# Projection stage of a transformer block on one core: PSUM pool layout, timing of the token statistics, spacing of staged loads, and staging tiles in two chunks

## The chip, the cores and the metric

The kernel runs as one program on one core of a Trainium2 chip. The metric is the device time of an execution in microseconds (us); three runs of the kernel before took 2074.11 to 2076.02 us, median 2075.82. The profile is one further execution, recorded by the hardware profiler. The engines are named as in the profile: PE (TensorE, matmul), PEld (its weight loads), DVE (VectorE), ACT (ScalarE), POOL (GpSimd), and SP, whose queue issues most of the DMA transfers. A "q" behind an engine's name (SPq, POOLq) is its instruction queue.

## The reference

A pre-norm transformer block on 2048 tokens of 640 features, 32 heads of 20, with a SwiGLU feed-forward part of 1728, all in float32:

```python
x = A_x
h = x + _A_ref(_layernorm(x, axis=-1), A_wqkv, A_wo)
h2 = h + _B_ref(_layernorm(h, axis=-1), B_w_gate, B_w_up, B_w_down)
```

`_A_ref` projects to q, k and v, takes softmax(q k^T / sqrt(20)) v for each head and multiplies by `wo`; `_B_ref` is (silu(z w_gate) * (z w_up)) w_down.

## The kernel before

**Stages.** The program has three stages in a row: the projections to q, k and v (up to 357 us), attention, and the feed-forward part with the output. The change edits the first one only. Tokens are worked off in four chunks of 512 (c = 0 to 3; the title's "chunks 2 and 3" are c = 1 and 2 here). To keep float32 accuracy, each operand is split into a high and a low part (`split`: ACT copies the high part, DVE or POOL subtracts), and each product is the sum of three products of such parts.

**Slots.** In each chunk the loop over `work` runs 18 slots (j = 0 to 17; slot number 18c + j): ten blocks of 128 columns of q or k (`query_key`), and eight half tiles of v (`value`). In chunk 0 the first two blocks are made together (`first_blocks`), and slot 1, `("none",)`, closes the first PSUM pools and opens others. A block is 15 matmuls, each cut into two halves of 64 rows of the array (`rounds`). The second half of a matmul is issued LAG = 19 matmuls behind its first half, so that first and second halves of different matmuls lie side by side on the array. At the start only first halves are there, at the end only second ones ("lone halves" in the text).

**From PSUM to DRAM.** A finished block is taken out of its PSUM bank by `keep`: before slot 10 ACT and DVE split it directly, later ACT copies it (line 605) into a staging tile e, POOL forms a difference of columns for keys (607), ACT makes the high part (85), POOL the low part (86), and a DMA stores it (500), issued by SP or, from slot 10 on, by POOL. `next_e` hands out the staging tiles in turn: two own ones and one in the space of `v_stk[0]`; in chunk 0, up to slot 10, also the two tiles that chunk 1's z will take. Values go through `keep_value` (649).

**Tokens of the next chunk.** `load_x(c)` issues four loads of 128 x 640 on SP (line 316). `norm(c)` returns 15 steps on DVE: four statistics (121, 122), seven pairs of small operations for the reciprocal root (95), four applications (460). The list `lns` is worked off one step at a time, at the ends of slots and in `visit`, which is called after each matmul of a block. From slot 11 or 12 on `flip` transposes the normalised tokens on PE and splits them into z.

**Maxima.** Softmax needs the largest score of each row ahead of attention. A part of these maxima is computed between the projections' matmuls: `max_four` (PE line 208, ReLU on ACT 220, maxima on DVE 230) from staged pieces of q and k, `max_pair` (188, 194) from the resident ones. The pieces come back from DRAM with `load_items` (DMA at line 148) into six tiles. PSUM holds 8 banks: before slot 1 two for the first blocks (`ps_one`) and three pairs for transposes (`ps_wide`); after it five for maxima and transposes (`ps_max`) and three for blocks (`ps_one`).

**What sets the order.** Each engine works off its instructions in the order in which they are written. A planner in the kernel chooses that order: `clock` holds an estimated time for each engine in ns, `takes` advances it, and `visit` writes the next step of maxima, of a split or of `lns` when these clocks allow. A staged load counts as landed LANDING = 8000 ns (12000 in early slots) after its issue on this clock. The clock is the planner's own guess and no measurement.

Of the kernel before, what the change touches and what calls it, by code (L numbers as in the profile page):

```python
# [9 lines left out]
F32 = mybir.dt.float32  # L10
# [7 lines left out]
P = 128  # L18
# [7 lines left out]
CH = 512  # L26
NC = S // CH
# [17 lines left out]
def tile_block(ctx: ExitStack, tc: tile.TileContext, x, wqkv, wo, wg, wu, wd, out):  # L45
# [22 lines left out]

    const = ctx.enter_context(tc.tile_pool(name="const", bufs=1))
    ps_ctx = ExitStack()  # L70
    psum = ps_ctx.enter_context(tc.tile_pool(name="psum", bufs=1, space=bass.MemoryType.PSUM))

    def ps_wide():
        return psum.tile([P, 2, CH], F32, name="ps_wide", tag="ps_wide", bufs=3)

    def ps_one():
        return psum.tile([P, CH], F32, name="ps_one", tag="ps_one", bufs=2)

    ident = const.tile([P, P], F32, name="ident")
    make_identity(nc, ident)  # L80
# [226 lines left out]
    with tc.tile_pool(name="pa", bufs=2) as pa:  # L307
# [18 lines left out]
        slot = [0]  # L326
# [14 lines left out]
        def load_items():  # L341
            for n, (which, g, c, loaded, _) in enumerate(items):
                if loaded is not None:
                    continue
                if slot[0] < stored_at(which, g, c) or (n >= 6 and users[n - 6]):
                    return
                if n % 6 >= 4:
                    t = more[n % 6 - 4]
                else:
                    t = raw_tile().rearrange("p a b -> p (a b)")[:, : 2 * CH].rearrange(  # L350
                        "p (h n) -> p h n", h=2
                    )
                stack(t, which, g, c, slice(CH // 2, EW) if which else slice(0, CH))
                items[n][3:] = t, clock["PE"] + (LANDING if slot[0] > 23 else LANDING_FIRST)
# [50 lines left out]
        early += staged(0, (2, 1), (2, 0))  # L405

        seconds, steps_due = [], [0]
        LANDING, LANDING_FIRST, SLACK, GATE = 8000, 12000, 0, 500

        def visit():  # L410

            load_items()
            pe = clock["PE"]
            if seconds and seconds[0][0] <= pe + SLACK:
                seconds.pop(0)[1]()
                return
            if splits and splits[0][0] <= pe and clock["ACT"] <= pe + 200:
                splits.pop(0)[1]()
            if steps_due[0] and lns and clock["DVE"] <= pe + 100:
                steps_due[0] -= 1  # L420
                lns.pop(0)()
            if held[1][0] > pe + SLACK or clock["ACT"] > pe + GATE:
                return
            for queue in (early, urgent) if slot[0] < 57 else (urgent, early):
                if queue and queue[0][0]():
                    last = queue.pop(0)[1]()
                    if last:
                        seconds.append(last)
                    return
# [245 lines left out]
        for m, raw in enumerate(first_raw):  # L675
# [1 line left out]
            nc.vector.tensor_tensor(  # L677
                out=w_lo[:, :, cs], in0=raw, in1=w_hi[:, :, cs].bitcast(F32), op=ALU.subtract
            )
        load_x(1)  # L680
        load_w(4)
        loaded = 5
        split_at = (0, 4, 6, 7, 8, 9, 10, 11, 12, 13)
# [6 lines left out]
        for c in range(NC):  # L690
            lns = []
            work = (some_keys + some_queries if c else first) + parts
            if c == NC - 1:
                work = some_keys + parts + some_queries

                es[:] = [e for e in es if e is not third]
                es.insert(1, z_tiles(NC)[0][:, :2])
            for j, (kind, *which) in enumerate(work):
                slot[0] = 18 * c + j
                if c == 0 and j < 9:  # L700
                    for i in range(split_at[j], split_at[j + 1]):
                        split_w(i + 2)
                        if i % 2 == 1 and loaded < 8:
                            load_w(loaded)
                            loaded += 1
                if (c, j) == (0, 0):
                    es[:0] = [
                        t.rearrange("p k n -> p (k n)")[:, : 2 * EW].rearrange(
                            "p (i n) -> p i n", i=2
                        )  # L710
                        for t in z_tiles(1)
                    ]
                if (c, j) == (0, 10):
                    es[:] = [e for e in es if any(e is own for own in own_es)]
                if j == 0 and c + 1 < NC:
                    if c > 0:
                        load_x(c + 1)
                    lns = norm(c + 1)
                if which:
                    if (c, j) == (0, 0):  # L720
                        first_blocks((0, 1), (1, 0), (1, 1), (0, 2), (1, 2))
                        for m, ps in enumerate(firsts):
                            keep(0, m, ps)
                    else:
                        (query_key if kind == "block" else value)(c, *which)
                else:
                    ps_ctx.close()
                    ps_ctx = ExitStack()
                    psum, psum_jobs = (
                        ps_ctx.enter_context(  # L730
                            tc.tile_pool(name=name, bufs=n, space=bass.MemoryType.PSUM)
                        )
                        for name, n in (("psum_p", 5), ("psum_j", 3))
                    )

                    def ps_one():
                        return psum_jobs.tile([P, CH], F32, name="ps_one", tag="ps_one")

                    def ps_max():
                        return psum.tile([P, CH], F32, name="ps_max", tag="ps_max")  # L740

                if c == 0 and j == 6:
                    for ev in evs:
                        nc.gpsimd.memset(ev, 1.0)
                if j == (5 if c == 0 else 4):
                    load_keys(0, slice(c * CH, (c + 1) * CH))
                if j == (5 if c == 0 else 9) and c < 3:
                    load_queries(c)
                if 0 in ends:
                    finish_at = min(finish_at, slot[0] + 2)  # L750
                    if slot[0] == finish_at:
                        max_finish(0)
                if j == 15 and c == 3:
                    load_values(0)
                if slot[0] < 9:
                    for _ in range(2 if j >= 5 else 1):
                        if j >= 1 and lns:
                            lns.pop(0)()
                else:
                    while steps_due[0] and lns:  # L760
                        steps_due[0] -= 1
# [1073 lines left out]
```

## Time and profile before

| what | us |
|---|---|
| median of three runs | 2075.82 |
| the profiled execution | 2072.07 |
| its span in the trace | 2070.1 |
| PE busy | 2031.9 (98%) |
| DVE busy | 1637.2 (79%) |
| ACT busy | 1437.0 (69%) |
| POOL busy | 745.3 (36%) |
| first / last projection matmul (line 527) starts | 26.0 / 356.2 |
| first matmul of attention (line 1127) starts | 357.3 |

How to read it: the trace lists instructions by engine with start, duration, source line, the tile written and the tiles read, the shape, and, where the engine idled before, for how long and which instruction released it. Buffer numbers are left out of names, so `e` is any of the staging tiles `e0`, `e1`. "Granted clock" is the share of full speed that PE was given; where it is 0.5, matmuls take twice as long and PE still counts as busy. Windows give busy time of each engine by stretch. Line numbers are those of the kernel before; behind the first edits the changed kernel's are higher by 4 to 13.

### The profile page before, as it was taken

Reading aid. Unit: us, or ns where it says so; the run is one execution under the profiler, and the core shown is the slowest. Engines: PE = TensorE matmul, PEld = TensorE weight load, DVE = VectorE, ACT = ScalarE, POOL = GpSimd, SP = SyncE. Lnnn points to the kernel's source line nnn. Section 1 sums busy time; section 2 is a strip of 40 time slices with the busy share of each in tenths; the row PEclk is TensorE's granted clock in tenths of the full one; section 3 lists DMA queues with packets and bytes.
Section 4 is the critical chain, followed back from the end, with each engine's and each line's share of the span. In section 5 each row is a group of like instructions: output and inputs, shape, how many; then the busy total and the mean of one; then the engine's idle time right before and its main releaser. Section 6 shows DMA issues by size and latency. Waiting matters only on the chain.

```text
span 2070.1 us, 39666 instructions
## 1 busy us (share of the span) xinstructions
PE 2031.9 (98%) x14198; PEld 1257.6 (61%) x14198; DVE 1637.2 (79%) x2895; ACT 1437.0 (69%) x2835; POOL 745.3 (36%) x1042
## 2 busy tenths in 40 slices
PE   7989999999999999999999999999999999999999
PEld 6878998333333333333333333345588888888888
DVE  6767777888888888888888888886368666676677
ACT  3647866999999999999999999996733222212221
POOL 2353533234344253344310010001145444754555
PEclk9999999999999999999999999999999999999999
DMA  6756744153443443534522113132138765884542
GB/s 208 245 186 204 217 149 134 44 177 107 144 131 121 154 132 104 186 118 164 159 86 75 36 47 95 30 109 63 32 132 304 238 193 166 320 290 160 198 150 96
DMA packets 192172, 305.53 MB, mean 148 GB/s; under 512 B 47440, under 2 KB 82256, under 8 KB 190952
## 3 DMA queue, kind: packets, MB, share of 16 engines
q1 hardware_dynamic: 185272, 278.34, 42.2%
q0 software_dynamic: 6608, 24.65, 3.8%
q8 instruction: 113, 1.85, 0.4%
q14 instruction: 83, 0.68, 0.1%
q10 hardware_dynamic: 96, 0.00, 0.0%
HBM read 203.82 MB, written 98.30 MB: 146 GB/s over the span
## 4 chain that ended last, share of the span: by engine, by line
PE 89%; DMA 4%; DVE 3%; POOL 1%; ACT 1%; issue 1%; SPq 1%; ACTq 0%; DVEq 0%; POOLq 0%
PE acc L1137 25%; PE ps_one L1127 16%; PE ps_a L1298 15%; PE ps_max L241 12%; PE ps_b L1392 8%; PE ps_one L527 7%; PE ps_max L208 2%; PE ps_max L858 2%; PE ps_b L858 1%; DMA halves<-j_d 1%; DVE mx L194 1%; DMA q_d<-e 1%; DMA xt<-in_A_x 1%; DMA units<-w_d 0%; DMA k_d<-v_stk 0%
## 5 line engine op out<-in xcount | busy, mean ns | idle before, releaser
L1133 ACT ACTIVATE probs<-ps_one 128x512 f32<-128x512 f32 x2048 | 1056.6, 613 | 62.2 <-PE ps_one L1127 37.1
L247 DVE TENSOR_REDUCE mx<-ps_max 128x1 f32<-128x512 f32 x1472 | 926.2, 684 | 109.6 <-PE ps_one L1127 74.4
L1127 PE MATMUL ps_one<-q_stk,k_stk 62*128 62x512 f32 x2048 | 586.0, 450 | 2.6 <-DVE m L86 1.8
L1137 PE MATMUL acc<-probs,v_stk 128*32 128x512 f32 x4096 | 545.2, 604 | 0.2 <-ACT o L1147 0.2
L1127 PEld LDWEIGHTS ps_one<-q_stk,k_stk 62*128 62x128 f32 x2048 | 251.3, 184 | 432.9 <-ACT probs L1133 397.3
L241 PE MATMUL ps_max<-k_stk,q_stk 60*128 60x512 f32 x1472 | 381.8, 425 | 0.0
L241 PEld LDWEIGHTS ps_max<-k_stk,q_stk 60*128 60x128 f32 x1472 | 271.7, 186 | 23.9 <-DVE mx L247 1.2
L1513 DVE TENSOR_TENSOR tmp<-ps_a,tmp 128x512 f32<-128x512 f32 x208 | 141.2, 690 | 120.5 <-PE ps_a L1298 94.6
L230 DVE TENSOR_REDUCE mx<-ps_max 128x2 f32<-128x512 f32 x256 | 161.7, 686 | 56.5 <-PE ps_max L208 48.3
L1172 POOL TENSOR_TENSOR o<-o,rb 128x512 f32<-128x512 f32 x31 | 39.9, 1288 | 411.1 <-DMA q_stk<-q_d 161.9
L1137 PEld LDWEIGHTS acc<-probs,v_stk 128*32 128x32 f32 x4096 | 80.5, 108 | 174.8 <-issue 166.0
L1392 PE MATMUL ps_b<-halves,yp 128*128 128x320 f32 x1032 | 179.3, 308 | 2.0 <-DMA halves<-j_d 1.2
L1392 PEld LDWEIGHTS ps_b<-halves,yp 128*128 128x128 f32 x1032 | 165.1, 188 | 18.6 <-POOL yp L86 1.5
L220 ACT ACTIVATE ps_max<-ps_max 128x512 f32<-128x512 f32 x256 | 135.8, 581 | 47.4 <-PE ps_max L208 41.2
L1298 PE MATMUL ps_a<-t,units 128*128 128x512 f32 x624 | 162.6, 396 | 0.0
L1298 PE MATMUL ps_a<-z,units 128*128 128x512 f32 x516 | 133.8, 394 | 0.0
L86 POOL TENSOR_TENSOR yp<-y,yp 128x256 fp32r<-128x256 f32 x96 | 60.3, 628 | 188.0 <-ACT yp L85 180.1
L1298 PEld LDWEIGHTS ps_a<-t,units 128*128 128x128 f32 x624 | 112.5, 188 | 18.6
L1397 DVE TENSOR_TENSOR h<-ps_b,h 128x320 f32<-128x320 f32 x248 | 110.0, 481 | 6.5 <-PE ps_b L1392 5.4
L527 PE MATMUL ps_one<-z_hi,w_hi 64*128 64x512 f32 x380 | 108.9, 410 | 5.7 <-DVE z_lo L86 2.9
L527 PE MATMUL ps_one<-z_hi,w_lo 64*128 64x512 f32 x380 | 108.8, 402 | 0.0
L527 PE MATMUL ps_one<-z_lo,w_hi 64*128 64x512 f32 x380 | 108.1, 405 | 0.0
(201 smaller groups left out, 2652.1 us busy)
## 6 DMA issues: line engine op xcount, KB each, us to landing
units<-w_d SPq DMA_DIRECT2D x186, 256.0 KB
w_d<-stage SPq DMA_DIRECT2D x106, 256.0 KB
halves<-j_d SPq DMA_DIRECT2D x70, 320.0 KB
j_d<-stage SPq DMA_DIRECT2D x42, 320.0 KB
k_stk<-k_d SPq DMA_DIRECT2D x64, 160.0 KB
q_stk<-q_d SPq DMA_DIRECT2D x64, 160.0 KB
raw<-k_d SPq DMA_DIRECT2D x54, 160.0 KB
rb<-r_d SPq DMA_DIRECT2D x32, 256.0 KB
```

Source lines behind the costliest of these rows:

```text
L220: nc.scalar.activation(ps, ps, AF.Relu)
L230: nc.vector.tensor_reduce(mx[:, b, :, t, kc], ps.rearrange("p (j n) -> p j n", j=2), axis=AX.X, op=ALU.max,)
L241: nc.tensor.matmul(ps, queries[u][rows, pair, t * P : (t + 1) * P], keys[u // NC][rows, pair, kc * CH : (kc + 1) * CH], start=True, stop=True,
L247: nc.vector.tensor_reduce(mxs[u][:, b, pair, t, kc : kc + 1], ps, axis=AX.X, op=ALU.max)
L527: nc.tensor.matmul(ps, a[rows], b[rows], start=(i == n == 0), stop=(i == 1 and n == last), skip_group_check=True,)
L1127: nc.tensor.matmul(ps, keys[u // NC][rows, p, kt * P : (kt + 1) * P], queries[u][rows, p, :], start=True, stop=True,)
L1133: nc.scalar.activation(probs[p][:, b, :], ps, AF.Exp, scale=scale)
L1137: nc.tensor.matmul(acc[32 * j : 32 * j + 32, :], values[u // NC][:, kt, j * VW : j * VW + 32], probs[j // 2][:, j % 2, :], start=(kt == 0) ...
L1298: nc.tensor.matmul(ps.rearrange("p (t n) -> p t n", t=TPC), w[k][:, i], z[k][:, :, j], start=(first and m == 0), stop=(last and m == len(n ...
L1392: nc.tensor.matmul(ps, a, b, start=(n == 0), stop=(n == len(pairs) - 1))
L1397: nc.vector.tensor_tensor(out=h, in0=ps, in1=h, op=ALU.add)
L1513: add = lambda out, ps, x: nc.vector.tensor_tensor(out=out, in0=ps, in1=x, op=ALU.add)
```

## The change

Four edits, all in the projection stage.

1. The first PSUM pool is divided in two. The two banks of the first blocks (`psum_two`) stay open to the end of the stage; only the pool of the transposes (`psum_wide`) is closed at slot 1. On its six banks stand three for blocks (`psum_j`) and three for maxima (`psum_p`); maxima take their banks in turn from the three and from the two that stayed.
2. The x of chunk 1 is loaded at slot 3 instead of before the loop. For all chunks the steps of `norm` are written only when PE's planned time is X_LANDING = 15000 ns past the issue of the load, and each step now counts 500 ns on DVE's planned time. Up to 2, from slot 8 on up to 4 steps are due per slot (before: 1 or 2). In chunk 0 this replaces fixed numbers per slot.
3. Two staged loads are at least APART = 2500 ns of PE's planned time apart.
4. In chunks c = 1 and 2, as in chunk 0 before, the two tiles of the next chunk's z serve as further staging tiles up to slot 10; they are taken after the three others.

```diff
-    psum = ps_ctx.enter_context(tc.tile_pool(name="psum", bufs=1, space=bass.MemoryType.PSUM))
+    flip_ctx = ExitStack()
+    psum_two, psum_wide = (
+        c.enter_context(tc.tile_pool(name=name, bufs=n, space=bass.MemoryType.PSUM))
+        for c, name, n in ((ps_ctx, "psum_o", 2), (flip_ctx, "psum_w", 3))
+    )
...
+                if clock["PE"] < next_load[0]:
+                    return
+                next_load[0] = clock["PE"] + APART
...
+        STEP, X_LANDING, x_there = 500, 15000, [0]
+        next_load = [0]
+
+        def norm_step():
+            lns.pop(0)()
+            takes("DVE", STEP, clock["PE"])
...
-            if steps_due[0] and lns and clock["DVE"] <= pe + 100:
+            if steps_due[0] and lns and clock["DVE"] <= pe + 100 and pe >= x_there[0]:
                 steps_due[0] -= 1
-                lns.pop(0)()
+                norm_step()
...
-        load_x(1)
         load_w(4)
...
-                if (c, j) == (0, 0):
+                if c + 1 < NC and j == 0:
                     es[:0] = [
...
-                        for t in z_tiles(1)
+                        for t in z_tiles(c + 1)
                     ]
-                if (c, j) == (0, 10):
+                    if c:
+                        es[:] = es[2:] + es[:2]
+                if c + 1 < NC and j == 10:
                     es[:] = [e for e in es if any(e is own for own in own_es)]
-                if j == 0 and c + 1 < NC:
-                    if c > 0:
-                        load_x(c + 1)
+                if j == (0 if c else 3) and c + 1 < NC:
+                    load_x(c + 1)
+                    x_there[0] = clock["PE"] + X_LANDING
                     lns = norm(c + 1)
...
-                    ps_ctx.close()
-                    ps_ctx = ExitStack()
-                    psum, psum_jobs = (
+                    flip_ctx.close()
+                    psum_jobs, psum = (
                         ps_ctx.enter_context(
-                            tc.tile_pool(name=name, bufs=n, space=bass.MemoryType.PSUM)
+                            tc.tile_pool(name=name, bufs=3, space=bass.MemoryType.PSUM)
                         )
-                        for name, n in (("psum_p", 5), ("psum_j", 3))
+                        for name in ("psum_j", "psum_p")
                     )
+                    turn = [0]
...
                     def ps_max():
-                        return psum.tile([P, CH], F32, name="ps_max", tag="ps_max")
+                        n = turn[0] % 5
+                        turn[0] += 1
+                        pool, tag = (psum, "ps_max") if n < 3 else (psum_two, "ps_two")
+                        return pool.tile([P, CH], F32, name="ps_max", tag=tag)
...
-                if slot[0] < 9:
-                    for _ in range(2 if j >= 5 else 1):
-                        if j >= 1 and lns:
-                            lns.pop(0)()
-                else:
+                if clock["PE"] >= x_there[0]:
                     while steps_due[0] and lns:
                         steps_due[0] -= 1
-                        lns.pop(0)()
-                    steps_due[0] = 2 if j >= 4 else 1
+                        norm_step()
+                    steps_due[0] = 4 if j >= 8 else 2
```

More of the change, by code (lines that the diff above doesn't have):

```diff
@@ L70, in tile_block @@
     ps_ctx = ExitStack()
-    psum = ps_ctx.enter_context(tc.tile_pool(name="psum", bufs=1, space=bass.MemoryType.PSUM))
+    flip_ctx = ExitStack()
[3 more added lines that the diff above has]
+    )
     def ps_wide():
-        return psum.tile([P, 2, CH], F32, name="ps_wide", tag="ps_wide", bufs=3)
+        return psum_wide.tile([P, 2, CH], F32, name="ps_wide", tag="ps_wide")
     def ps_one():
-        return psum.tile([P, CH], F32, name="ps_one", tag="ps_one", bufs=2)
+        return psum_two.tile([P, CH], F32, name="ps_two", tag="ps_two")
     ident = const.tile([P, P], F32, name="ident")
@@ L407, in tile_block @@
         seconds, steps_due = [], [0]
-        LANDING, LANDING_FIRST, SLACK, GATE = 8000, 12000, 0, 500
+        LANDING, LANDING_FIRST, SLACK, GATE, APART = 8000, 12000, 0, 500, 2500
+        STEP, X_LANDING, x_there = 500, 15000, [0]
[3 more added lines that the diff above has]
+            takes("DVE", STEP, clock["PE"])
         def visit():
```

## The prediction

> **What bounds the kernel now.** First the page, for which engine runs without gaps and where.
>
> ```profile
> span 2070.1 us, 39666 instructions
> ...
> PE 2031.9 (98%) x14198; PEld 1257.6 (61%) x14198; DVE 1637.2 (79%) x2895; ACT 1437.0 (69%) x2835; POOL 745.3 (36%) x1042
> ...
> PE   7989999999999999999999999999999999999999
> ```
>
> TensorE (PE) is busy for 98% of the span. The gaps lie in the first few slices of 51.8 us, the part that the change edits: projections and the maxima woven between them, up to 357 us. Behind it the slices are full, and every engine's order there is the same in both programs, so a gain in the first part moves the rest forward by as much. PE's own work stays the same; what can shrink is its idle time and the stretches at a lower granted clock (the 40 slices hide these). Second view: what PE waited for up to 370 us, in total, times, longest.
>
> ```profile
> PE ps_max L208 <- DVE mx L230: 7.4, 2, 5.7
> PE ps_one L527 <- DVE z_lo L86: 2.9, 2, 2.6
> PE ps_one L527 <- ACT e L605: 2.5, 2, 1.8
> ...
> PE ps_max L208 <- DMA raw<-q_d: 0.5, 1, 0.5
> ```
>
> The first three rows hold most of it (the wait for the first x, 8 us, stays). I then read each in the timeline and in windows of 2 us (columns: stretch, length, busy PE, PEld, DVE, ACT, POOL, granted clock, DMA share, GB/s).
>
> **Part 1: the PSUM pool that stays open.**
>
> ```profile
> 20.45 3.03 DVE L86 TENSOR_TENSOR w_lo<-raw,w_hi 128x640 fp32r<-128x640 f32 x4
> ...
> 25.26 0.69 DVE L86 TENSOR_TENSOR z_lo<-ps_one,z_lo 128x512 fp32r<-128x512 f32 x1
> ...
> 26.01 1.56 PE L527 MATMUL ps_one<-z_hi,w_hi 64*128 64x512 f32 x5 [2.61 <-DVE z_lo L86]
> ...
> 41.67 0.49 PE L527 MATMUL ps_one<-z_hi,w_hi 64*128 64x512 f32 x1 [0.28 <-DVE e L86]
> ```
> ```profile
> 26.00:28.00 2.00, 1.99 (x7) 1.60 (x8) 2.00 (x4) 1.73 (x3) 0.00 (x0) 0.79 1.02 349
> ...
> 30.00:32.00 2.00, 2.00 (x6) 1.58 (x5) 0.00 (x0) 0.00 (x0) 0.00 (x0) 0.50 0.97 306
> ...
> 36.00:38.00 2.00, 2.00 (x15) 1.57 (x13) 0.00 (x0) 0.00 (x0) 0.00 (x0) 0.65 0.00 0
> ```
>
> At 26.01 PE has waited 2.61 us for VectorE (DVE) to read the second of the two first blocks (z_lo<-ps_one, ends 25.95). The pools are closed and reopened at that point, and the new job pool lies on the banks of those blocks. In the changed program the two banks stay with them and the new job pool takes three banks of the transposes. Its first product waits only for the last transpose and for w_hi of its own block, its eleventh for that block's w_lo (first of the four splits from 20.45). All are done before 23.4, where the gap begins. Term: 2.6 us (bounds 2.0 to 2.6).
>
> The gap has a second price. The granted clock is 0.79 at 26 to 28 us, so half speed began about 27.2 (0.21/0.5 of 2 us, 0.84 us before 28); it is 0.50 until 36, and 0.65 at 36 to 38, so full speed is back after 1.4 us of it. That is 0.8+8.0+1.4 = 10.2 us at half speed with PE busy throughout, so 5.1 us of it are lost. Whether all of it returns depends on the stream behind the gap: 19 lone first halves on 64 of 128 rows, before the second halves join them (LAG). The clock returned only after these were through. At the end of the projections such a lone stream stands at full clock:
>
> ```profile
> 355.26 1.33 PE L527 MATMUL ps_one<-z_hi,w_lo 64*128 64x512 f32 x5
> ```
> ```profile
> 354.00:356.00 2.00, 2.00 (x11) 1.55 (x10) 0.14 (x1) 0.43 (x1) 1.29 (x1) 1.00 0.46 131
> ```
>
> There the clock stays 1.00, and five lone halves take 1.33 us, the last of them 0.39 (row 121.08 below), so one follows the other after (1.33-0.39)/4 = 0.235 us. Nineteen are 4.5 us. I take the full 5.1 us; bounds 0 and 5.1.
>
> The Trainium skill, "TensorE: Matmul & The Clock Gate", Part 1, says that the array falls to half clock after an idle window of about 3.4 us and is back at full after about 3.4 us of sustained matmuls, and that the window runs freely. The trace disagrees twice: here a gap of 2.61 us, further down one of 1.81 us, was enough, and the return took 10.2 us. By the page's figure the half-clock term would be 3.4/2 = 1.7 us, and the whole sum 3.4 us smaller; the measured stretch decides.
>
> **Part 2: the load of x for chunk 1, and its statistics.** Four issues on SP's queue move from before the later weight loads to slot 3, behind the weights and the first key store, ahead of a query store.
>
> ```profile
> 28.32 2.64 SPq L500 DMA_DIRECT2D q_d<-z_lo  x2
> 42.67 1.27 SPq L500 DMA_DIRECT2D k_d<-e  x3
> ```
>
> SP has issued nothing between 30.96 and 42.67 us, so four issues fit there; what stands behind them (the query store q_d<-z_lo) is needed only at 53 us. Cost 0. The four statistics, though, now stand within about two blocks, where DVE also splits weights and copies blocks out. Each costs 0.89+0.21 = 1.1 us (rows of part 3). The row at 41.67 shows that a copy-out which is late by nothing already costs PE 0.28 us, so one statistic ahead of a copy-out can cost up to 1.1 us, twice. Bounds 0 and 2.2; I take 0.6 lost, nearer to nothing, as two of the four are ahead of no copy-out.
>
> **Part 3: statistics await their landing.** This is the largest stall.
>
> ```profile
> 99.30 2.75 SPq L316 DMA_DIRECT2D xt<-in_A_x  x4
> ```
> ```profile
> 106.35 0.89 DVE L121 BATCH_NORM_STATS2 st<-xt 128x6 f32<-128x320 f32 x2 [6.27 <-DMA xt<-in_A_x]
> 107.27 0.21 DVE L122 BATCH_NORM_AGGREGATE mv<-st 128x2 f32<-128x12 f32 x1
> ```
> ```profile
> 108.10 0.79 PE L208 MATMUL ps_max<-raw,raw 60*128 60x256 f32 x3 [5.72 <-DVE mx L230]
> ```
> ```profile
> 104.00:106.00 2.00, 0.00 (x0) 0.00 (x0) 0.00 (x0) 0.00 (x0) 0.00 (x0) 0.91 0.99 268
> ...
> 110.00:112.00 2.00, 2.00 (x16) 1.95 (x16) 1.93 (x7) 1.07 (x2) 0.00 (x0) 0.50 0.00 0
> 112.00:114.00 2.00, 2.00 (x22) 1.85 (x20) 1.92 (x4) 0.89 (x2) 0.00 (x0) 0.88 0.00 0
> ```
>
> The x of chunk 2 (counting from 0) is issued at 99.30, lands by 106.35, 7.05 us later, and the first statistic, queued ahead of the maxima on the in-order DVE, holds these 6.27 us; PE runs out of free banks and idles 5.72 us. Clock 0.88 at 112 to 114 means half speed to 112.5, so from 108.1 on 4.4 us at half, 2.2 us lost. Together 7.9 us.
>
> In the changed order 54 half products and 38 matmuls of maxima stand between the place of the first issue of x and the first statistic. Two half products run side by side, so one costs half of 0.235, 0.117 us; what four matmuls of maxima cost, two rows show:
>
> ```profile
> 120.84 0.50 PE L208 MATMUL ps_max<-raw 60*128 60x256 f32 x4
> 121.08 0.39 PE L527 MATMUL ps_one<-z_hi,w_hi 64*128 64x512 f32 x1
> ```
>
> 0.24 us, 0.06 each. So 54 x 0.117 + 38 x 0.06 = 8.6 us against 7.05 us: the data is there 1.5 us ahead, more if SP runs ahead of PE. What replaces the wait: two of the four statistics still go back to back ahead of maxima. Nearest row, of the next chunk, three back to back:
>
> ```profile
> 194.28 0.88 DVE L121 BATCH_NORM_STATS2 st<-xt 128x6 f32<-128x320 f32 x2
> ...
> 196.31 0.83 DVE L121 BATCH_NORM_STATS2 st<-xt 128x6 f32<-128x320 f32 x2
> ...
> 198.00 0.50 PE L208 MATMUL ps_max<-raw 60*128 60x256 f32 x3 [1.63 <-DVE mx L230]
> ```
>
> That cost PE 1.63 us for 3.3 us of DVE. I take 0.4 off for two: 7.5 us, bounds 5.7 (clock not recovered) and 7.9. In the next chunk the three become single ones with maxima between, two adjacent: 1.1 of the 1.63 us return, bounds 0 and 1.6.
>
> **Part 4: more staging tiles, and maxima that move.**
>
> ```profile
> 134.29 0.76 POOL L607 TENSOR_TENSOR v_stk<-v_stk 128x256 f32<-128x256 f32 x1
> ...
> 139.88 0.74 POOL L607 TENSOR_TENSOR e<-e 128x256 f32<-128x256 f32 x1
> ```
> ```profile
> 140.65 0.84 ACT L85 ACTIVATE e<-e 128x768 fp32r<-128x768 f32 x1 [4.24 <-POOL e L607]
> 141.40 0.58 ACT L605 ACTIVATE e<-ps_one 128x512 f32<-128x512 f32 x1
> ...
> 146.51 0.60 ACT L605 ACTIVATE v_stk<-ps_one 128x512 f32<-128x512 f32 x1 [3.87 <-DMA k_d<-v_stk]
> ```
> ```profile
> 142.03 0.50 PE L527 MATMUL ps_one<-z_hi,w_hi 64*128 64x512 f32 x1 [1.81 <-ACT e L605]
> ```
> ```profile
> 144.00:146.00 2.00, 2.00 (x16) 1.65 (x14) 2.00 (x4) 0.00 (x0) 1.98 (x3) 0.50 0.92 289
> ```
>
> The stall of 1.81 us at 142.03 (and 0.7 shortly before, the other of the two waits in the third row of PE's waits) is that of the key blocks of chunk 1. It looks like a lack of staging tiles, but isn't: ScalarE (ACT) empties the bank at 141.40 because its queue stood 4.24 us before the split at 140.65, which waits for GpSimd (POOL). POOL needs 5.6 us per key block (134.29 to 139.88: difference, split, store issues), a block on PE 30 x 0.117 = 3.5 us. More tiles do not shorten that. What they remove is ACT's wait at 146.51, 3.87 us for a store to land; PE pays nothing for it but later maxima. The spaced loads push 24 more matmuls of maxima, 24 x 0.06 = 1.4 us of PE work, into these blocks, which would cover half the stall, but their ReLUs also stand ahead of ACT's split of block 1, and so delay POOL. I take one for the other, term 0. Bounds: +4.2 (2.5 idle and half of the half-clock stretch behind, some 3.4 us, all gone) and -2 (the delay without the cover).
>
> **Part 5: spacing of the staged loads, and the end.** Two four-head steps end later, among the last lone halves, so DVE's last maxima end after PE instead of before.
>
> ```profile
> 351.45 2.69 DVE L230 TENSOR_REDUCE mx<-ps_max 128x2 f32<-128x512 f32 x4 [0.57 <-PE ps_max L208]
> ```
> ```profile
> 357.32 0.56 PE L1127 MATMUL ps_one<-q_stk,k_stk 62*128 62x512 f32 x2 [0.74 <-ACT e L605]
> ```
>
> Two reductions are half of 2.69, 1.35 us, behind the last product; today PE waits 0.74 us there for ACT. Lost 0.6 us, bounds 0 and 1.4. From there on every engine has the same order as before.
>
> **Sum.** 2.6 + 5.1 - 0.6 + 7.5 + 1.1 + 0 - 0.6 = 15.1 us. The profiled execution took 2072.1 us (span 2070.1) and would take 2057.0. The median of the runs shown is 2075.8, 3.7 above it; the change takes the same time off both, so I forecast 2075.8 - 15.1 = 2060.7 us.
>
> **The rivals.** (a) The clock falls all the same: the lone halves right behind the transposes count as half activity. For: it did not come back during them at 27 to 34 us. Against: 354 to 356 us. Loses 2.6 to 5.1 of the 5.1: about 2064.7.
>
> (b) The landing is met too late or the maxima stall elsewhere: DVE, with 4.4 us of statistics among maxima in chunk 1, becomes the bound there, and half of part 3 is given back, with half clock behind the new gap, 3.7 + 1.7 us: about 2066. For: the 1.63 us row. Against: 1.5 us of margin.
>
> (c) The change doesn't do what it says at the first pool: something else holds PE at 23.4, and part 1 brings nothing: 2075.8 - 7.4 = 2068.4. Against: what its first product awaits, above.
>
> (d) Slower: staged loads come late, all of them. A load is taken as landed 8 us after the planner's issue, and SP issues in order.
>
> ```profile
> 80.54 1.89 SPq L148 DMA_DIRECT2D raw<-q_d  x4
> ```
> ```profile
> 87.23 0.47 PE L208 MATMUL ps_max<-raw 60*128 60x256 f32 x3 [0.54 <-DMA raw<-q_d]
> ```
>
> Here one took 6.7 us from issue to landing and cost PE 0.54 us. Loads that are spaced are each used nearer to their landing. Were all of some 25 first uses late by 1.2 us, PE would lose 30 us, and the time be 2075.8 - 15.1 + 30 = 2090.7. It decides from about 0.6 us per use on (15.1/25). Against: with the loads in bursts this is the only one in the view of PE's waits, and spacing shortens the queue ahead of each.
>
> **Chances.** Forecast (gain of 11 to 21) 0.50; (a) 0.20; (b) 0.14; (c) 0.04; a mixture that ends within 0.2% (4.2 us, about what a measurement of this kernel tells from no change) 0.06; (d) 0.06. Faster 0.88, same 0.06, slower 0.06. The upper end of gain is the forecast with part 4's 4.2 and 1.0 for smaller waits, 20.3: 2055; measured against the profiled execution's level it is 2052. The other end takes in (a), (b) and (c): 2070. The forecast's own range is 2055 to 2064.
>
> **What would show it.** Right: no wait of PE at its first L527 product; clock 1.00 from 24 to 40 us; no DMA wait of the statistics at about 95 us and no half clock behind; PE still waiting for ACT in the key blocks of chunk 1, with POOL at 5 to 6 us a block; projections that end at about 342 us. Wrong: a half-clock stretch near 28 us (a), a new wait of maxima for DVE at chunk 1's start (b), many waits for raw loads (d), or projections that end early while the total doesn't follow.

## The result, and the profile after

| what | before, us | after, us |
|---|---|---|
| median of four runs each, same chip | 2075.92 | 2053.96 |
| the profiled execution | 2072.07 | 2053.55 |
| its span | 2070.1 | 2051.7 |
| first matmul of attention starts | 357.32 | 339.64 |

The ratio of the times is 0.9897, with a 95% interval of 0.988 to 0.9914: the change takes 22.0 us off the median, where 15.1 were forecast. 2053.96 us lies 1.0 us below the forecast's own range of 2055 to 2064 and inside the wide one, 2052 to 2070. A second measurement of both kernels, further down, gives 19.2 us. The page of the changed kernel:

```profile
span 2051.7 us, 39661 instructions
...
PE 2025.1 (99%) x14198; PEld 1252.2 (61%) x14198; DVE 1640.7 (80%) x2895; ACT 1436.3 (70%) x2835; POOL 745.0 (36%) x1042
```

What PE waited for from 16 to 370 us (total, times, longest; line numbers are now 4 to 13 higher: 212 was 208, 234 was 230, 540 was 527, 618 was 605):

```profile
PE ps_max L212 <- DVE mx L234: 2.0, 4, 0.8
PE ps_one L540 <- ACT v_stk L618: 1.8, 1, 1.8
PE ps_one L1140 <- ACT e L618: 0.9, 1, 0.9
PE ps_one L540 <- ACT z_lo L618: 0.7, 1, 0.7
```

The waits of 5.7 us (for maxima) and 2.6 us (for z_lo) are gone; those of the key blocks for ACT stay. The first product after the first blocks, in the timeline of PE and in windows of 2 us (busy PE, PEld, DVE, ACT, POOL, then granted clock, DMA share, GB/s):

```profile
20.52 2.56 PE L593 MATMUL ps_two<-z_hi,w_lo 128*128 128x256 f32 x20
23.01 1.42 PE L540 MATMUL ps_one<-z_hi,w_hi 64*128 64x512 f32 x5
```
```profile
24.00:26.00 2.00, 2.00 (x10) 1.58 (x9) 1.81 (x3) 2.00 (x6) 0.74 (x1) 1.00 0.90 273
...
28.00:30.00 2.00, 2.00 (x20) 1.63 (x18) 0.54 (x1) 0.18 (x1) 0.00 (x0) 1.00 0.99 360
```

It starts at 23.01 instead of 26.01, with no gap in brackets behind the row, and the clock stays 1.00 where it was 0.50. The statistics of chunk 2 (SP's queue, DVE, PE):

```profile
87.60 2.32 SPq L320 DMA_DIRECT2D xt<-in_A_x  x4
```
```profile
106.01 0.88 DVE L125 BATCH_NORM_STATS2 st<-xt 128x6 f32<-128x320 f32 x2
...
109.19 0.88 DVE L125 BATCH_NORM_STATS2 st<-xt 128x6 f32<-128x320 f32 x2
```
```profile
108.74 0.50 PE L212 MATMUL ps_max<-raw 60*128 60x256 f32 x3 [0.27 <-DVE mx L234]
```

The x is issued at 87.60, 18.4 us ahead of its first use, and DVE no longer waits for it; of the 5.72 us stall 0.27 is left. The key blocks of chunk 1:

```profile
114.92 0.75 POOL L620 TENSOR_TENSOR e<-e 128x256 f32<-128x256 f32 x1
...
120.03 0.76 POOL L620 TENSOR_TENSOR z_hi<-z_hi 128x256 f32<-128x256 f32 x1
...
125.56 0.74 POOL L620 TENSOR_TENSOR z_lo<-z_lo 128x256 f32<-128x256 f32 x1
```
```profile
122.20 0.49 PE L540 MATMUL ps_one<-z_hi,w_hi 64*128 64x512 f32 x1 [0.74 <-ACT z_lo L618]
127.72 0.49 PE L540 MATMUL ps_one<-z_hi,w_hi 64*128 64x512 f32 x1 [1.76 <-ACT v_stk L618]
```

POOL still begins a key block every 5.1 to 5.5 us, the new staging tiles (z_hi, z_lo) are in use, and PE still waits 0.74 and 1.76 us there.

To set all this side by side, the stage is cut into six stretches. From windows of half a microsecond each cell gives PE's idle time and, behind the plus, the time that it lost at half clock while busy (busy time times what the granted clock lacks to 1). The columns are places in the program, not equal work: each later stretch of a faster kernel begins a little further on.

| kernel, execution | 16-40 | 40-94 | 94-118 | 118-150 | 150-290 | 290-366 | sum |
|---|---|---|---|---|---|---|---|
| before, first | 2.6+5.1 | 3.2 | 5.7+2.2 | 2.9+1.7 | 3.4 | 1.8 | 28.6 |
| before, second | 2.6+3.4 | 3.0 | 5.0+1.9 | 3.4+1.6 | 2.6+1.7 | 1.8+3.4 | 30.4 |
| after, first | 0 | 2.5 | 0.3 | 2.5+1.7 | 1.5 | 1.9 | 10.4 |
| after, second | 0 | 2.7 | 0.3 | 2.5+1.7 | 1.0 | 1.9+3.4 | 13.5 |
| PSUM alone, first | 0.3 | 3.0 | 5.0+2.4 | 2.8+1.7 | 3.5 | 1.7+3.4 | 23.9 |
| PSUM alone, second | 0.3 | 3.2 | 5.5+1.9 | 3.4+1.7 | 3.8 | 1.7+3.4 | 25.0 |
| gap filled | 0.6 | 3.1 | 5.3+2.7 | 4.9 | 3.2+1.7 | 1.8+3.4 | 26.7 |
| x alone | 2.5+5.1 | 1.2 | 1.3 | 3.4 | 3.4 | 1.7+1.7 | 20.3 |
| PSUM and x | 0 | 2.2 | 1.6 | 2.4+1.7 | 2.1 | 1.7+1.7 | 13.4 |
| no spacing, first | 0 | 1.2 | 0.8 | 0.5 | 2.1 | 1.8 | 6.5 |
| no spacing, second | 0 | 1.3 | 0.8 | 0.6 | 1.8 | 1.7+1.7 | 7.9 |

Between the first two profiled executions the sums differ by 18.2 us, and the spans by 18.4: for this pair the table holds the whole gain. What lies behind the stage, the same in all kernels, varies by itself: from the first matmul of attention to the end it takes 1712.0 to 1715.8 us in the 14 traces, and 0.9 to 2.7 us more in one execution than in the other of the same kernel. The total of a single execution can't be read more closely than that.

### The profile page after: what moved, and what is told of

Its sections match the earlier page's. It is cut to its first block, busy times and chain, and to the rows that moved or that the text cites. A ratio compares the mean times of both kernels' runs of the same rounds, so it can differ in the third digit from the quotient of the medians.

```text
span 2051.7 us, 39661 instructions
## 1 busy us (share of the span) xinstructions
PE 2025.1 (99%) x14198; PEld 1252.2 (61%) x14198; DVE 1640.7 (80%) x2895; ACT 1436.3 (70%) x2835; POOL 745.0 (36%) x1042
## 4 chain that ended last, share of the span: by engine, by line
PE 92%; DVE 2%; DMA 2%; POOL 1%; ACT 1%; issue 1%; SPq 1%; ACTq 0%; DVEq 0%; POOLq 0%
PE acc L1150 25%; PE ps_one L1140 16%; PE ps_a L1311 15%; PE ps_max L245 12%; PE ps_one L540 8%; PE ps_b L1405 8%; PE ps_max L212 3%; PE ps_max L871 2%; PE ps_b L871 1%; DVE mx L198 1%; DMA halves<-j_d 1%; PE ps_max L492 0%; DMA raw<-k_d 0%; PE ps_two L593 0%; DMA o_t<-o_d 0%
## 5 line engine op out<-in xcount | busy, mean ns | idle before, releaser
L224 ACT ACTIVATE ps_max<-ps_max 128x512 f32<-128x512 f32 x256 | 135.1, 579 | 39.9 <-PE ps_max L212 32.6
```

Of the source, the lines that this page charges most:

```text
L224: nc.scalar.activation(ps, ps, AF.Relu)
```

## The experiments

Three jobs, each on a chip of its own and with its own runs of the kernel before (medians 2072.47, 2074.05 and 2074.16 us). Ratios are to those; what follows rests on ratios within a job or on the traces.

**One edit at a time.** The kernel before with the PSUM edit alone (edit 1 of the diff above):

> The kernel before with the PSUM edit alone (two pools, only the wide one closed at slot 1, maxima over 3+2 banks). Theory (gap and half clock both belong to the closed pool): no wait of PE at its first product of 64 rows, clock 1.00 from 24 to 40 us, 2.6 + 5.1 = 7.7 us less than before, about 2068.2. Rival 1 (the clock falls by itself in the stream of products of 64 rows): only the gap goes, 2.6 us less, about 2073.3. Rival 2 (what starts earlier waits at the next stall, the statistics at 106 us, because their data lands no earlier): under 2 us less, about 2075; the stall of 6.27 us there would then be longer by what was gained.

Measured: 2069.8 us against 2072.47, ratio 0.9985 (0.9975 to 0.9995), 2.7 us instead of 7.7. Both things that the theory named at this place came out: no gap, full clock, 0.3 us left of 7.7. But the total did not follow by as much. The kernel before with the edit of x alone (edit 2):

> The kernel before with the edit of x alone (load of chunk 1 in slot 3, statistics 15000 ns behind their issue on the planner's clock, four steps a visit from j = 8 on). Theory: stall of 5.72 us and the half clock behind it go, 7.5 + 1.1 - 0.6 = 8.0 us less, about 2067.9; the first gap at 26 us and its half clock stay. Rival: part of the stall moves to later maxima, as statistics in a row still hold the vector engine: 4 us less, about 2072. With the pool run, the sum of both gains should be that of the run that has both, if the edits don't need each other.

Measured: 2063.22 us, ratio 0.996 (0.9947 to 0.9972), 9.3 us against 8.0 forecast. Its trace has the first gap and its half clock as before, and no stall at the statistics. Both together:

> The kernel before with the PSUM edit and the edit of x, without spacing and without more staging tiles. Theory (these two carry the whole change): 7.7 + 8.0 = 15.7 us less, about 2060; with what the changed kernel gained beyond the forecast counted to the small waits that went with them, down to 2054. Rival (spacing or tiles carry the 5 to 7 us by which the changed kernel beat the forecast): not below 2060.

Measured: 2054.31 us, ratio 0.9919 (0.9907 to 0.9932), 18.2 us. So the two edits carry nearly the whole change (0.9897 and 0.9905 in its two measurements), and the PSUM edit, worth 2.7 us alone, is worth 8.9 on top of the edit of x. The two don't add up: 2.7 + 9.3 = 12.0. By the means of the same executions it is 3.5 + 9.4 = 12.9 against 17.8, which is 4.9 us apart (2 to 8, an estimate from the scatter of the executions). This rests on the times. The few traces don't show it: the first matmul of attention starts 4.3 us earlier with the PSUM edit (mean of two traces of each kernel), 8.8 us earlier with the edit of x and 13.8 us earlier with both (one trace each).

**The gap or its clock.** The kernel before, with its gap filled by products that nobody reads:

```diff
                         for m, ps in enumerate(firsts):
                             keep(0, m, ps)
+                        warm = ps_wide()
+                        for k in range(10):
+                            nc.tensor.matmul(
+                                warm[:, 0, :], w_hi[:, k % ND, :P], zs[0][0][:, k % ND, :],
+                                start=True, stop=True,
+                            )
```

> The kernel before with its gap kept but filled: ten products of 128 rows by 512 columns, which nobody reads, into a bank of the wide pool just before the pools change. They take about 10 x 0.25 = 2.5 us of the 2.61 us. Theory (half clock is the price of the idle gap): the first product of 64 rows still starts at about 26.0 us, but the clock stays 1.00 behind it, 5.1 us less than before, about 2070.8. Rival (the stream of 64 rows itself lowers the clock): no gain, about 2075.9, half clock from about 27 to 37 us as before.

Measured: 2069.65 us, ratio 0.9985 (0.9975 to 0.9995), 2.8 us less. Its timeline of PE, and two windows:

```profile
23.28 2.49 PE L726 MATMUL ps_wide<-z_hi,w_hi 128*128 128x512 f32 x10
26.08 1.40 PE L527 MATMUL ps_one<-z_hi,w_hi 64*128 64x512 f32 x5 [0.31 <-DVE z_lo L86]
```
```profile
26.00:28.00 2.00, 1.92 (x8) 1.59 (x9) 2.00 (x4) 2.00 (x4) 0.00 (x0) 1.00 0.92 314
30.00:32.00 2.00, 2.00 (x20) 1.63 (x20) 1.76 (x4) 0.00 (x0) 0.00 (x0) 1.00 0.99 307
```

The first product starts at 26.08, where it did, and behind it the clock is 1.00 in the same stream of products of 64 rows. So the idle gap lowers the clock, not the stream, and the clock can be kept without moving the work. But this kernel and the PSUM edit gain the same: a front that is 5 to 8 us shorter shows up in the medians as less than 3 (in the means as 3.8 and 3.5).

**Where it went: a second execution of the same kernels.**

> The kernel before, unchanged, for a second profiled execution. Theory (the stalls are set by the order of work and recur, but which of them lowers the clock depends on where they fall in a grid that runs by itself): stalls of about 2.6, 5.7 and 1.8 us at the same places within 1 us, but the stretches of half clock at other places or of other lengths than 27.2 to 37.4, 105.6 to 112.5 and 143.2 to 146.6, and further ones, such as at the end of the projections; 10 to 17 us lost in all. Rival (a gap lowers the clock by its length alone): the same three stretches, within 0.5 us.

> The kernel before with the PSUM edit alone, a second profiled execution (the first was the shortest of 11). Theory: full clock from 24 to 40 us again, the stall of the statistics still there (5 to 6 us), half clock behind it longer than or equal to that of the first look; 8 to 12 us lost in all. Rival (the first look was typical): the same three stretches at 98, 136 and 351 us, within 1 us.

Measured: 2071.13 and 2070.43 us. In the second execution of the kernel before, the stalls recur (2.61, 4.96 and 2.73 us; the last two end 2.2 and 1.7 us earlier than in the first execution, more than the 1 us of the theory). The half clock stands behind them again, at 27.7 to 34.5, 102.8 to 109.6 and 140.4 to 143.8, the first time for 6.8 us instead of 10.2, and also at 195.0 to 198.4 and 355.4 to 362.2, where the first execution had none. That is 12.1 us lost with PE busy, inside the theory's 10 to 17; the rival's same three stretches did not come. With the PSUM edit alone, the stretches of both executions are alike but for the last, which lies 3.6 us later: the rival held at two places of three. This pair can't tell the two ideas apart, since its grids (next paragraph) happen to lie only 0.17 us from each other.

Within the stage the stretches last 3.4, 6.8 or 10.2 us, one, two or three times 3.41, and within an execution they begin whole multiples of 3.41 us apart (first execution of the kernel before: 27.16, 105.64 and 143.20; 23 and 11 steps). Between executions this grid is shifted. So the grid can be laid over each trace, and each of its windows read as one row. Kernel before, first execution, then second:

```profile
23.75:27.16 3.41, 1.15 (x5) 0.97 (x6) 2.65 (x5) 3.32 (x7) 0.73 (x1) 1.00 0.93 290
27.16:30.58 3.42, 3.42 (x10) 2.64 (x9) 1.99 (x5) 1.31 (x2) 0.00 (x0) 0.50 1.07 366
...
139.80:143.22 3.42, 1.61 (x14) 1.06 (x12) 1.03 (x2) 1.96 (x3) 2.45 (x3) 1.00 0.90 330
...
61.30:64.71 3.41, 1.95 (x18) 1.44 (x18) 3.41 (x7) 0.14 (x1) 0.00 (x0) 1.00 0.94 288
194.41:197.82 3.41, 1.96 (x21) 1.54 (x17) 3.31 (x10) 1.46 (x4) 0.54 (x1) 1.00 0.71 206
```
```profile
191.56:194.98 3.42, 1.79 (x19) 1.42 (x17) 3.32 (x10) 0.86 (x3) 0.54 (x1) 1.00 0.77 228
194.98:198.39 3.41, 3.41 (x23) 3.41 (x21) 1.90 (x4) 1.99 (x4) 0.00 (x0) 0.50 0.63 203
351.99:355.40 3.41, 2.67 (x14) 1.91 (x14) 0.00 (x0) 1.15 (x3) 2.92 (x4) 1.00 0.35 81
```

A window in which PE is busy for 1.15 or 1.61 of 3.41 us is followed by half clock; one of 1.95 or 1.96 is not. The same stall near 195 us leaves 1.96 us of busy time in the one execution's window and 1.79 in the other's, and only there does the clock fall. Over the 14 traces, and windows at full clock from 16 us on and ahead of the end of the projections: at 48% busy or less, half clock followed each time (17 windows); at 49 to 58%, in 3 of 13; from 60% on, never. (The clock's first record in a trace stands at 11 to 14 us.) The end is an exception: windows of 72 to 83% busy, filled with products of 62 to 64 rows, are followed by half clock in 11 of 14 executions, for 1.7 or 3.4 us of loss. This bears out rival (a)'s mechanism (lone halves count for less) at another place, before and after alike.

The number of products in a window sorts better than its busy time. PE is as busy with one half product as with two side by side, and at half clock it is busy longer with each. Changed kernel behind its first blocks, then the kernel before, the next two windows behind the gap:

```profile
23.19:26.60 3.41, 3.41 (x16) 2.70 (x16) 2.65 (x5) 3.14 (x6) 0.74 (x1) 1.00 0.97 296
```
```profile
30.58:33.99 3.41, 3.41 (x14) 2.64 (x14) 1.78 (x4) 0.00 (x0) 0.00 (x0) 0.50 0.76 256
33.99:37.40 3.41, 3.41 (x19) 2.65 (x18) 0.00 (x0) 0.00 (x0) 0.00 (x0) 0.50 0.00 0
```

Count each product by its share of 128 rows and of 512 columns, and by the part of its record that lies inside the window (the transposes against `ident` twice, since they begin 0.11 to 0.13 us apart for 128 columns, where lone halves of 512 columns begin 0.235 us apart). These windows then hold 7.1 whole products (full clock, which stays), 5.9 (half clock, which stays) and 8.1 (half clock, which ends); the one at 27.16 holds 4.1. In all 14 traces there are 8255 windows at full clock from 16 us to just before the end of the span. With 6.12 whole products or fewer, half clock followed in 31 of 32, the eleven at the end of the projections among them; with 6.16 or more it never did, and the three ends that kept the clock hold 6.2 to 6.4. A stretch of half clock goes on where a window holds 6.04 or fewer (12 windows) and ends from 6.2 on, but for four windows at the start of attention. The boundary was found in these same traces, and nearly all products of the stage have 60 to 64 rows, so that rows and number of products are hard to tell apart; no run varied them by themselves.

The Trainium skill, "TensorE: Matmul & The Clock Gate", Part 1, says that the array is watched in a window of 4096 cycles, 3413 ns, which runs freely; the grid of 3.41 us agrees, and explains the 10.2 us at which the prediction saw a disagreement: three windows, not one long return. Its condition for the fall, an idle window, is too strict here: 48% of busy time was little enough.

So a stall's price in clock depends on where the grid lies in an execution. Summed over an execution, it is its span times what the mean granted clock lacks to 1; the clock is listed to three places, so this is good to 1 us in one execution. The 21 executions of the kernel before in the first job lost 10.3 to 16.6 us in this way. The means over all timed executions of that job:

| kernel | executions | mean time, us | of it lost at half clock | the rest |
|---|---|---|---|---|
| before | 21 | 2072.7 | 12.7 | 2060.0 |
| PSUM alone | 11 | 2069.2 | 10.3 | 2058.9 |
| gap filled | 11 | 2068.9 | 8.8 | 2060.1 |
| x alone | 5 | 2063.3 | 8.7 | 2054.6 |
| PSUM and x | 5 | 2054.9 | 2.9 | 2052.1 |

Here idle time at half clock counts as lost too. The gap that was only filled leaves the rest as it was and takes 3.9 us from the clock's part: that is its price by this measure, against 5.1 in the one profiled execution and 3.4 in the other. PSUM and x take 9.8 from the clock's part, and 2.4 + 4.0 alone: with one edit, the other stalls and the end go on costing clock. Why they cost more then than in the kernel before, by 3.4 us in the mean, stays open; in the traces of the PSUM edit alone it is the end (3.4 in both).

**Without the staging tiles of chunks 1 and 2** (edit 4 undone):

> The changed kernel without the extra staging tiles in chunks 1 and 2 (those of chunk 0 stay). Theory (key blocks are paced by POOL, not by tiles): 2054.0, within 1 us of the changed kernel, waits of PE for ACT in the key blocks of chunk 1 as before. Rival (tiles carry part of the gain beyond the forecast): 2056 to 2058, with ACT waiting for stores to land (3.9 us before) and PE behind it.

Measured: 2055.5 us against 2074.05, ratio 0.9915 (0.9902 to 0.9929), no difference from the changed kernel that can be told. Its waits for ACT in the key blocks total 3.1 us (2.3 at most) instead of 2.5: the tiles are worth half a microsecond of idle there.

**The pace of GpSimd.** The difference of the key blocks on the vector engine, then the stores of chunk 1's key blocks on SyncE, each in the changed kernel:

```diff
-                    nc.gpsimd.tensor_tensor(
+                    nc.vector.tensor_tensor(
                         out=over, in0=copy[:, :half], in1=copy[:, half:CH], op=ALU.subtract
```
```diff
                     if not sync:
-                        store()
+                        store(queue=nc.sync if which and c == 1 else nc.gpsimd)
```

> The changed kernel with the difference of the key blocks (256 columns) on the vector engine in place of GpSimd. Theory (GpSimd sets the pace of chunk 1's key blocks, 5.5 us a block against 3.5 us on PE): 0.74 us and the wait for it leave GpSimd, its cadence falls to about 3.8 us, the waits of 0.74 and 1.76 us at 122 and 128 us go, and the half clock behind them (about 1.6 us lost): 3 to 4 us less than the changed kernel, about 2050.5. Rival (the vector engine, in order, waits for ScalarE's copies and holds maxima): no gain or up to 2 us more, 2054 to 2056.

> The changed kernel with the stores of chunk 1's key blocks issued by SyncE in place of GpSimd. Theory (GpSimd sets the pace): 1.2 to 1.7 us of issue per block leave it, cadence about 4.0 us, the stall of 1.76 us and its half clock go: 2 to 4 us less than the changed kernel, about 2051. Rival (SyncE waits in order for GpSimd's splits and issues the staged loads behind them late): waits for raw loads appear, 2055 to 2060.

Measured: 2055.45 us, ratio 0.9911 (0.9897 to 0.9924), and 2062.18 us, ratio 0.994 (0.9928 to 0.9953). GpSimd in the first, then in the second:

```profile
118.33 1.84 POOL L90 TENSOR_TENSOR e<-e 128x768 fp32r<-128x768 f32 x1 [1.04 <-ACT e L89]
121.89 1.84 POOL L90 TENSOR_TENSOR z_hi<-z_hi 128x768 fp32r<-128x768 f32 x1 [0.18 <-ACT z_hi L89]
...
125.74 1.85 POOL L90 TENSOR_TENSOR z_lo<-z_lo 128x768 fp32r<-128x768 f32 x1
```
```profile
114.87 0.74 POOL L620 TENSOR_TENSOR e<-e 128x256 f32<-128x256 f32 x1
...
118.38 0.74 POOL L620 TENSOR_TENSOR z_hi<-z_hi 128x256 f32<-128x256 f32 x1
```

Its pace falls from 5.1-5.5 us to 3.6-3.9 and to 3.5, and in both the waits of PE for ACT in the key blocks are gone. So GpSimd did set the pace. Neither kernel gained the 2 to 4 us of its theory, though: both rivals came true as well, at another place, the second with 2 us more than its range. DVE and PE in the first (timelines), and PE's waits in the second (total, times, longest):

```profile
107.84 0.42 DVE L620 TENSOR_TENSOR e<-e 128x256 f32<-128x256 f32 x1 [1.18 <-ACT e L618]
108.18 0.88 DVE L125 BATCH_NORM_STATS2 st<-xt 128x6 f32<-128x320 f32 x2
```
```profile
110.91 0.79 PE L212 MATMUL ps_max<-raw 60*128 60x256 f32 x3 [1.88 <-DVE mx L234]
```
```profile
PE ps_max L212 <- DMA k_d<-z_lo: 4.3, 1, 4.3
...
PE ps_max L212 <- DMA raw<-q_d: 1.7, 2, 1.0
PE ps_max L212 <- DMA raw<-k_d: 1.1, 1, 1.1
```

On the vector engine the difference waits 1.18 us for ScalarE's copy, ahead of the statistics, and the maxima behind them hold PE for 1.88 us: the wait moved. On SyncE the staged loads share the queue with stores that wait for GpSimd, and PE waits 7.1 us in these rows, where the changed kernel waits 0.3 us for DMA in the same view: 4.3 us at once, which the profile puts down to the landing of a store, and 2.8 us for staged loads.

**Without spacing** (edit 3 undone in the changed kernel), twice, the second time beside the changed kernel:

> The changed kernel without the 2500 ns between staged loads. Theory (spacing is worth nothing in itself, it costs some 0.6 us at the end): 2053.4 to 2054.0. Rival (spacing removed the small waits of maxima and of raw loads, 0.5 to 1.5 us each, and so the gain beyond the forecast): 2056 to 2058, with waits for raw loads back.

> The changed kernel, unchanged, beside its form without spacing on one chip. Theory (spacing delays the splits of the first key blocks and the maxima that would cover the wait behind them): 2054.0, 1 to 2 us above the form without spacing; the wait of 1.8 us for ScalarE at 128 us recurs, with or without half clock behind it. Rival (the difference of the first measurements was chance): within 0.5 us of the form without spacing.

> The changed kernel without the 2500 ns between staged loads, beside the changed kernel on one chip. Theory: 2052 to 2053, 1 to 2 us less than the changed kernel, no wait for ScalarE above 0.5 us in the key blocks of chunk 1. Rival: no difference, 2054, and the wait is there in this execution.

Measured: 2052.38 us against 2074.05, ratio 0.9896 (0.9883 to 0.991); then 2054.13 against 2054.93 us for the changed kernel, both ratios 0.9905 (0.989 to 0.992, and 0.9889 to 0.9922). The times show no difference. The traces do, in both executions: 6.5 and 6.2 us of idle time against 8.7 and 8.4, a first matmul of attention that starts 2.5 and 3.7 us earlier, and no wait of 1.76 us. PE's longest wait for a key block, then ScalarE and GpSimd without spacing:

```profile
PE ps_one L537 <- ACT v_stk L615: 0.3, 1, 0.3
```
```profile
104.84 1.07 ACT L224 ACTIVATE ps_max<-ps_max 128x512 f32<-128x512 f32 x2 [0.47 <-PE ps_max L212]
105.81 0.85 ACT L89 ACTIVATE e<-e 128x768 fp32r<-128x768 f32 x1
```
```profile
105.03 0.75 POOL L617 TENSOR_TENSOR e<-e 128x256 f32<-128x256 f32 x1
106.74 1.84 POOL L90 TENSOR_TENSOR e<-e 128x768 fp32r<-128x768 f32 x1 [0.96 <-ACT e L89]
110.60 0.74 POOL L617 TENSOR_TENSOR e<-e 128x256 f32<-128x256 f32 x1
```

and in the changed kernel:

```profile
107.69 1.07 ACT L224 ACTIVATE ps_max<-ps_max 128x512 f32<-128x512 f32 x2 [0.45 <-PE ps_max L212]
109.16 1.07 ACT L224 ACTIVATE ps_max<-ps_max 128x512 f32<-128x512 f32 x2 [0.41 <-PE ps_max L212]
110.13 0.85 ACT L89 ACTIVATE e<-e 128x768 fp32r<-128x768 f32 x1
```
```profile
108.15 0.74 POOL L620 TENSOR_TENSOR e<-e 128x256 f32<-128x256 f32 x1
111.06 1.85 POOL L90 TENSOR_TENSOR e<-e 128x768 fp32r<-128x768 f32 x1 [2.17 <-ACT e L89]
114.92 0.75 POOL L620 TENSOR_TENSOR e<-e 128x256 f32<-128x256 f32 x1
```

With spacing, more maxima are left for the first key blocks; four of their ReLUs (L224) instead of two stand ahead of ScalarE's split of the second block, GpSimd waits 2.17 us for it instead of 0.96, and its chain of five blocks, which sets PE's pace afterwards, runs later by that. From the third block on its pace is the same in both, 5.1 to 5.7 us, so the pace alone doesn't make PE wait. What spacing costs in the stage, 2.5 and 3.7 us here, is no more than the rest of an execution varies by, and no version was shown to beat the changed kernel in time.

## Why the prediction was right, point by point

**Part 1, first gap and clock (2.6 + 5.1).** Right in the traces: 7.7 and 6.0 us in the two executions, now 0. The size of the clock's term was one draw: 10.2 us at half clock in the first execution, 6.8 in the second. What the term is worth in the total depended on the other stalls, 2.7 us alone and 8.9 behind the edit of x (3.5 and 8.4 by the means), which the plain sum did not foresee.

**Part 2, statistics of chunk 1 (-0.6).** Not found as a loss: the stretch from 40 to 94 us has 2.5 to 2.7 us of idle time, 3.0 to 3.2 before. A misjudged size, 1 us. With the edit of x alone the stretch has 1.2, with both edits 2.2; what makes the difference stays open.

**Part 3, statistics that await their landing (7.5 + 1.1).** Right: the stretch of chunk 2's stall went from 7.9 and 6.9 to 0.3, and the stretch from 150 to 290 us, with the next chunk's, by 1.9 in the first executions; the next chunk's wait itself went from 1.63 to 0.80 us, 0.8 of the forecast 1.1. The margin was wrong on the safe side: 18.4 us from issue to use, where 8.6 had been worked out, since SP's queue runs ahead of PE.

**Part 4, staging tiles (0).** Right: without the tiles the time is the same. Its reason, GpSimd's pace, is shown from two sides, since the waits go when its work does; but they go without spacing too, at the same pace, so it takes a late start as well. The other half of the term, maxima that move into these blocks, had been set to zero as cover and delay; the delay is what the traces show when spacing is undone, while the times can't tell.

**Part 5, the end (-0.6).** PE waits 0.9 instead of 0.74 us, a loss of 0.2.

**The sum.** The first traces of the two kernels differ by 18.2 us, 3.1 more than the forecast, mostly small waits in the stretches from 40 to 94 and from 150 to 290 us. The rest of the miss is the step from the profile to the median: "the change takes the same time off both". It does not. The profiled execution of the kernel before lay 3.8 us below its median, that of the changed kernel 0.4 below. Part of this is chance: the kernel before has medians of 2072.47 to 2074.16 us in the three jobs above, and 2075.92 in this set of runs; beside each other in the third job the two kernels differ by 19.2 us. Part of it is the clock. The mean clock of the kernel before was 0.993 to 0.995 in most executions, of the changed one 0.998 to 0.999: with fewer stalls there are fewer windows in which the clock can fall. In the third job, by the measure of the table above, half clock fell from 13.6 to 3.6 us and the rest by 8.8, where the forecast has 7.3 (5.1 + 2.2) and 7.8. The term of the sum that was mis-sized most is the clock's, read from one execution.

**The rivals.** (a) did not occur at the first gap, but its mechanism shows at the end of the projections. There the prediction's row against (a), full clock from 354 to 356 us, was one of three exceptions in 14 executions: the forecast was right about the first gap, but on evidence that was luck. (b) did not occur (0.27 us), (c) is refuted by the first product at 23.01, (d) by the waits for raw loads, 0.3 us in all in the changed kernel. What (d) describes does exist: with stores on SyncE the time is 6.7 us above that of the kernel without tiles, in the same job.

## What to carry to other kernels

Price a stall of PE not by its length alone, but by how few products, counted by rows and columns, it leaves in a stretch of 3.4 us around it; one profile shows one draw of that price, so look at the mean granted clock of all timed executions before adding it to a sum. Edits that remove stalls need not add up: measure them together, and one on top of the other. Where an engine sets the pace of a chain, taking work off it helps only if the engine or the queue that takes it over has nothing behind that work which PE waits for.

## What the runs showed of the hardware

The clock of PE changes on a grid of 3.41 us whose place differs between executions of the same program. A window that was 48% busy was enough to lower it; windows 72 to 83% busy did so at the end of the projections, where only half of the rows were in use. In these 14 traces 6.1 whole products (128 rows by 512 columns) in a window are the boundary, with one exception in 8255. Of three windows in a row at half clock behind the first gap, two were busy throughout with products of 64 rows, and the clock did not return (4.1 and 5.9 whole products); the same stream stayed at full clock when it began there (7.1 in the window from 23.19 us of the changed kernel).
